# Sparse attention, then a layer-normed feed-forward block: a new order for the prologue and for each batch's attention pieces

## Chip, cores and metric

The kernel runs on one core of one Trainium2 chip. The metric is the device time of one execution in microseconds (us). Before the change it is 962.87 us, the median of three runs (959.76 to 963.36).

## The reference

Attention with 8 batches, 8 heads, 576 tokens and 64 values to a head. Heads 0 to 3 see the last 32 tokens (local), heads 4 to 7 see every 32nd token back (strided). Its result x (8 x 576 x 512) goes through a layer norm and a feed-forward block of 512 to 2048 to 512, and is added back:

```python
scores = scale * np.matmul(q, k.transpose(0, 1, 3, 2))
mask_local = (rel >= 0) & (rel < 32)
mask_strided = (rel >= 0) & (pos[None, :] % 32 == pos[:, None] % 32)
attn = softmax(np.where(masks, scores, -1e9))
x = attn @ v                                   # heads side by side: (8, 576, 512)
xn = (x - mu) / np.sqrt(var + 1e-06) * g_ln
out = x + np.maximum(xn @ w_ch1, 0.0) @ w_ch2
```

q, k and v are 32-bit floats; the two weight matrices are 64-bit floats.

## The kernel before

**Feed-forward.** The 8 x 576 tokens are cut into nine chunks of 512: chunk c below 8 is the first 512 tokens of batch c, the ninth is the 64 tokens left over from each batch. A chunk takes 16 steps f, one for each 128 columns of the hidden layer. A step has two halves on TensorE: `ffn1(c, f)` (L544) makes `ph` by 12 matmuls of 128x512 out of x and the first weights; ScalarE and VectorE turn `ph` into the two parts `hh` (L559) and `hl` (L560); `ffn2(c, f)` (L564) adds 12 more matmuls into the four outputs `po`. Everything is held as a high and a low part, hence three products for each. In the loop `ffn2` runs one step late: step f does `ffn1(c, f)`, an attention piece, `ffn2(c, f - 1)`. In chunk 0 there is one PSUM bank for `ph`; from chunk 1 on, when the bank of the weight preparation `ps_r` is given back, there are two. `finish` (L574) ends a chunk: it scales `po` with the row statistics `rs`, adds x and stores.

**Weights.** All weights stay in SBUF, and they are prepared on the way, one step's worth (`Split(f)`, L180) at a time: `scaled`, `low` (ScalarE), `magnitude`, `sign` (VectorE) turn 64-bit words into floats; `by_g`, `chunks_sum` (GpSimd) scale by g and sum over rows; `column_mean` (TensorE, L227, the tile `cm`) and `centred` (VectorE, L230) take off the column mean, which is the layer norm's mean; `two_parts` (ScalarE L241, GpSimd L242) makes high and low parts. During chunk 0 three splits are in work at a time: in step f the old one (f + 1) is ended, the next (f + 2) is in its middle, the one after (f + 3) is begun. Chunk 0 is the only chunk that carries this work.

**Attention.** A batch is four pairs of heads, in the order local, strided, local, strided; pair i of 32 belongs to batch i // 4. A pair goes through a turn (`t_piece`, L347: VectorE transposes q and k; `turned(i)`, L671, then issues the load of pair i + 1 on the SP queue) and four pieces: s (scores on TensorE into the one two-bank tile `ps_a`; mask L394, maximum L401 on VectorE; subtraction L406 on GpSimd; later the exponential L411 on ScalarE), p (transposes, copy L419), v (times v, L430 or L439; division L445 to L451 on VectorE; stores and the load of the next v on the SP queue), x (transposes L472 into `px`, split into the tiles `xh` L489 and `xl` L491 that the next chunk's `ffn1` reads). Below s5 is the s piece of pair 5. The generator `pieces` (L677) strings them as s(i+1), v(i), p(i+1), x(i), one for each step, across the batches' borders; a chunk's x must be ended when the chunk begins. Steps 0 and 1 of chunk 0 take no piece, so steps 12 to 15 take two each (L785 to L787), and chunk 0 takes 18 in all: s4 and p4, then up to s8, v7, p8, x7. The 32nd pair's x comes accordingly two steps before the end of chunk 6. Turns in chunk 0 stand at steps 0, 3, 5, 7, 8, 12, 14 (pairs 4 to 10).

**Prologue.** Batch 0's four pairs a, b, c, d (b and d strided) have no chunk to hide in. Lines 609 to 662 write out their order by hand, with the splits of weights 0 and 1 put between them. `t_rows` (L307) does the turn on TensorE, and four copies each on ScalarE and VectorE put the result in place (L325 local, L330 strided: 288 values to a row, written 36 values apart). Three two-bank tiles are handed round (`bank`, L249).

Each engine runs its instructions in the order in which they are written; a dependency at the end (L801 to L811) keeps it so.

## Time and profile before

| | |
|---|---|
| median of three runs | 962.87 us (959.76 to 963.36) |
| the profiled execution | 962.91 us |
| its span, first to last instruction | 961.1 us |
| TensorE busy | 923.6 us, 96% |
| VectorE / ScalarE / GpSimd busy | 391.5 / 225.2 / 143.1 us |
| mean granted clock of TensorE | 0.986 |

The profiled execution lies within 0.04 us of the median, and 1.8 us of it lie outside the span. Busy shares are means over the whole run; the tables of the busy tenths show VectorE, ScalarE and GpSimd at 5 to 8 tenths in the first sixth of the span, where the prologue and chunk 0 lie, and at 1 to 4 tenths after it, with TensorE at 9 or more. So the run has two parts that have to be read apart.

### The profile page before, as it was taken

The page shows a single profiled execution, that of the slowest core. Times are in us where ns is not written, and L with a number is a line of the kernel's source. Part 1 is how long each engine was busy: PE and PEld are TensorE (multiplying, and loading weights), DVE is VectorE, ACT ScalarE, POOL GpSimd, SP SyncE. Part 2 cuts the span into 40 slices and gives each one's busy share as a digit, 9 for nine tenths or more (in the row PEclk, how much of TensorE's full clock was granted, in tenths as well). Part 3 has the DMA queues.
Part 4 walks back from the last instruction along what each step waited for, and adds up shares of the span by engine and source line. Part 5 has one row for each costly group of instructions (what it writes and reads, how often), then busy time and mean ns, then how long its engine had stood idle before and what let it go on. Part 6 is the DMA issues. An engine that isn't in the chain of part 4 may idle for free.

```text
span 961.1 us, 18676 instructions
## 1 busy us (share of the span) xinstructions
PE 923.6 (96%) x7984; PEld 752.8 (78%) x7984; DVE 391.5 (41%) x685; ACT 225.2 (23%) x375; POOL 143.1 (15%) x180
## 2 busy tenths in 40 slices
PE   6679889999999999999999999999999999999996
PEld 5558677888888888888888888888888888888885
DVE  6668785433442344333442344334422321122112
ACT  5467562212121111121112111211112111101100
POOL 3368664000100010000000010001000000000000
PEclk9799998999999999999999999999999999999999
DMA  9997954524334242414432434243311121002001
GB/s 195 246 233 189 196 156 88 135 52 74 76 84 75 47 87 79 75 40 92 105 63 51 95 63 105 52 92 65 81 27 38 34 92 40 1 1 88 0 1 44
DMA packets 241666, 80.72 MB, mean 84 GB/s; under 512 B 192304, under 2 KB 234928, under 8 KB 241584
## 3 DMA queue, kind: packets, MB, share of 16 engines
q1 hardware_dynamic: 238688, 78.35, 36.1%
q10 hardware_dynamic: 2896, 1.18, 0.7%
q8 instruction: 63, 1.03, 0.5%
q14 instruction: 19, 0.16, 0.1%
HBM read 60.03 MB, written 19.46 MB: 83 GB/s over the span
## 4 chain that ended last, share of the span: by engine, by line
PE 88%; DVE 4%; issue 3%; POOL 2%; ACT 1%; DMA 1%; SPq 1%; DVEq 0%; ACTq 0%; POOLq 0%
PE po L570 40%; PE ph L551 26%; PE ph L555 13%; PE pp L416 2%; PE px L472 1%; PE av L430 1%; PE sp L375 1%; PE av L439 1%; PE sp L387 1%; DVE p L200 1%; SPq L292 1%; POOL w L242 1%; DVE r L206 1%; DVE kt_s L330 1%; DMA rows<-in_k_dram 1%
## 5 line engine op out<-in xcount | busy, mean ns | idle before, releaser
L570 PE MATMUL po<-w,hh 128*128 128x512 f32 x1152 | 367.5, 400 | 0.5 <-ACT hh L559 0.5
L560 DVE SCALAR_TENSOR_TENSOR hl<-ph,hh 128x512 fp32r<-128x512 f32 x144 | 99.6, 692 | 490.2 <-ACT hh L559 490.2
L570 PEld LDWEIGHTS po<-w,hh 128*128 128x128 f32 x1152 | 208.1, 188 | 43.3 <-ACT hh L559 0.7
L551 PE MATMUL ph<-xh,w 128*128 128x512 f32 x576 | 229.0, 398 | 0.0
L551 PE MATMUL ph<-xl,w 128*128 128x512 f32 x576 | 226.9, 394 | 0.0
L570 PE MATMUL po<-w,hl 128*128 128x512 f32 x576 | 225.6, 392 | 0.0
L559 ACT ACTIVATE hh<-ph 128x512 fp32r<-128x512 f32 x144 | 85.9, 596 | 567.8 <-PE ph L555 567.4
L555 PE MATMUL ph<-xh,w 128*128 128x512 f32 x576 | 155.6, 392 | 0.0
L570 PEld LDWEIGHTS po<-w,hl 128*128 128x128 f32 x576 | 108.1, 188 | 24.8 <-DVE hl L560 0.4
L551 PEld LDWEIGHTS ph<-xh,w 128*128 128x128 f32 x576 | 109.6, 190 | 22.6
L555 PEld LDWEIGHTS ph<-xh,w 128*128 128x128 f32 x576 | 109.3, 190 | 23.0
L551 PEld LDWEIGHTS ph<-xl,w 128*128 128x128 f32 x576 | 109.8, 191 | 22.3
L406 POOL TENSOR_TENSOR sm<-sm,mx 128x640 f32<-128x640 f32 (+1 forms) x32 | 40.7, 1271 | 406.4 <-DVE mx L401 403.0
L532 POOL TENSOR_TENSOR rs<-rs,mhalf 128x1 f32<-128x1 f32 x36 | 19.8, 550 | 360.6 <-DVE rs L531 360.6
L411 ACT ACTIVATE sm<-sm 128x640 f32<-128x640 f32 (+1 forms) x32 | 23.8, 744 | 98.2 <-POOL sm L406 98.2
L242 POOL TENSOR_TENSOR w<-r,w 128x512 fp32r<-128x512 f32 x32 | 40.9, 1293 | 28.9 <-ACT w L241 27.4
L491 DVE TENSOR_TENSOR xl<-px,xh 128x512 fp32r<-128x512 f32 (+2 forms) x48 | 30.1, 658 | 17.7 <-ACT xh L489 17.7
L576 DVE SCALAR_TENSOR_TENSOR x<-po,rs,x 128x512 f32<-128x512 f32 x36 | 24.7, 746 | 18.0 <-PE po L570 18.0
L489 ACT ACTIVATE xh<-px 128x512 fp32r<-128x512 f32 (+2 forms) x48 | 27.6, 650 | 10.7 <-PE px L472 9.9
L451 DVE TENSOR_TENSOR xo<-av,den 128x640 f32<-128x640 f32 (+1 forms) x32 | 28.5, 891 | 1.1
L472 PE MATMUL px<-ident,xo 128*128 128x128 f32 x160 | 24.4, 287 | 4.0 <-DVE xo L451 3.9
L200 DVE SCALAR_TENSOR_TENSOR p<-s,p 128x512 uint32<-128x512 uint32 x32 | 22.2, 693 | 12.8 <-ACT p L195 12.7
(73 smaller groups left out, 569.8 us busy)
## 6 DMA issues: line engine op xcount, KB each, us to landing
s<-in_moe_w_ch_dram SPq DMA_DIRECT2D x32, 512.0 KB
out_dram<-x SPq DMA_DIRECT2D x32, 256.0 KB
raw<-in_q_dram SPq DMA_DIRECT2D x112, 72.0 KB
raw<-in_k_dram SPq DMA_DIRECT2D x112, 72.0 KB
xds<-xo SPq DMA_DIRECT2D x32, 162.0 KB
v_l<-in_v_dram SPq DMA_DIRECT2D x32, 144.0 KB
v_l<-in_v_dram SPq DMA_DIRECT2D x32, 136.0 KB
xdl<-xo SPq DMA_DIRECT2D x16, 256.0 KB
```

Of the source, the lines that this page charges most:

```text
L200: nc.vector.scalar_tensor_tensor(out=self.p[i], in0=self.bits[i][:, :, 1], scalar=3, in1=self.p[i], op0=ALU.logical_shift_left, op1=ALU.bi ...
L242: nc.gpsimd.tensor_tensor(out=t[:, 1], in0=w, in1=t[:, 0].bitcast(F32), op=ALU.subtract)
L406: nc.gpsimd.tensor_tensor(out=sm, in0=sm, in1=mx[:, :, 0:nt].unsqueeze(3).broadcast_to([P, 2, nt, w]), op=ALU.subtract)
L451: nc.vector.tensor_tensor(out=xo[:, 0:nt].rearrange("p t h d -> p h t d"), in0=av[:, :, :, 0:D], in1=den.unsqueeze(3).broadcast_to([P, 2, ...
L472: nc.tensor.transpose(px[:, P * t:P * (t + 1)], self.xov[:, t], ident)
L489: nc.scalar.activation(out=dst(xh), in_=src, func=AF.Copy)
L491: nc.vector.tensor_tensor(out=dst(xl), in0=src, in1=dst(xh).bitcast(F32), op=ALU.subtract)
L551: nc.tensor.matmul(ph, w1h[:, cc], x[:, cc, :], start=(n == 0), stop=False)
L555: nc.tensor.matmul(ph, w1l[:, cc], xh[:, cc, :], start=False, stop=(cc == NCC - 1))
L559: nc.scalar.activation(out=hh, in_=ph, func=AF.Relu)
L560: nc.vector.scalar_tensor_tensor(out=hl, in0=ph, scalar=0.0, in1=hh.bitcast(F32), op0=ALU.max, op1=ALU.subtract)
L570: nc.tensor.matmul(po[i], hx[:, cs], w, start=(f == 0 and n == 0), stop=(f == NFC - 1 and n == 2))
```

## The change

What it does, part by part:

1. `t_rows`, strided: the copy walks the same 288 values in the other order, so that it writes runs of 18 neighbours and reads PSUM 16 values apart.
2. The prologue's order: split 0 is spread over the pairs' work (`d.s_act` earlier, `scaled(1)`, `low(1)`, `column_mean`, `centred` and `two_parts` between the p, v and x pieces), split 1 is begun before d's v piece, and its `column_mean` is done in the prologue.
3. Step 0's `ph` is begun in the prologue, pair by pair: 3 matmuls for pair a's rows ahead of d's x piece, 9 after it, in the order b, c, d.
4. Step 0 takes the turn of pair 4 and no `ffn2`; `ffn2(0, 0)` moves to step 1, behind `ffn1(0, 1)` and ahead of s4.
5. A batch's attention is 16 pieces within one chunk. In chunk 0: s4 at step 1, none at 2, p4, s5, v4, p5, x4, s6, v5, p6, x5, s7, v6 at steps 3 to 13, p7 and x6 at 14, v7 and x7 at 15. Turns at steps 0, 3, 6, 10, 14 and 15 (pairs 4 to 9; the last stands behind x7). Later chunks: one piece for each step, s, s, p, v, p, x, s, v, p, x, s, v, p, x, v, x.
6. Chunk 0's loads of x move from steps 9 to 12 to steps 11 to 14, and its row statistics from steps 11 to 14 (one each) to 14 and 15 (two each). Other chunks keep theirs.

```diff
-                            t = dst[rows, 0:S].rearrange("p (u c t) -> p c t u", c=2, t=NB)
-                            copy(out=t[:, c], in_=src.rearrange("p (t u) -> p t u", u=n))
+                            t = dst[rows, 0:S].rearrange("p (u c t) -> p c u t", c=2, t=NB)
+                            copy(out=t[:, c], in_=src.rearrange("p (t u) -> p u t", u=n))
...
+    def ffn1_part(c, f, ph, ccs):
+        xh, xl = xt[c]
+        w1h, w1l = w1_parts(f)
+        for cc in ccs:
+            for w, x in ((w1h, xh), (w1l, xh), (w1h, xl)):
+                nc.tensor.matmul(
+                    ph, w[:, cc], x[:, cc, :], start=(cc == 0 and x is xh and w is w1h),
+                    stop=(cc == NCC - 1 and x is xl))
...
-    new.scaled(0)
-    new.low(0)
-    new.scaled(1)
-    new.magnitude(0)
-    new.sign(0)
-    new.by_g()
-    new.chunks_sum()
+    s0.scaled(0)
+    s0.low(0)
+    s0.magnitude(0)
+    s0.sign(0)
+    d.s_act()
+    s0.scaled(1)
+    s0.by_g()
+    s0.chunks_sum()
     a.v_piece()
+    s0.low(1)
+    c.p_piece()
+    s0.magnitude(1)
+    s0.sign(1)
     b.v_piece()
+    d.p_piece()
+    s0.column_mean()
+    s0.centred()
+    c.v_piece()
     a.x_piece()
...
+    s0.two_parts(0)
     b.x_piece()
...
+    s1 = Split(1)
+    s1.scaled(0)
+    s1.low(0)
+    d.v_piece()
+    s1.magnitude(0)
+    s1.sign(0)
+    s0.two_parts(1)
+    s1.by_g()
+    s1.chunks_sum()
     c.x_piece()
...
+    s1.scaled(1)
+    ph0 = ffn1_ph(0, 0)
+    ffn1_part(0, 0, ph0, (0,))
     d.x_piece()
+    ffn1_part(0, 0, ph0, (2, 1, 3))
+    s1.low(1)
+    s1.magnitude(1)
+    s1.sign(1)
+    s1.column_mean()
     pairs[NHP].load_v()
     pairs[NHP + 1].load_v()
     w_late()
...
+    def pieces(i):
+        p = pairs[i:i + NHP]
+        s, t, u, x = ([getattr(p, n) for p in p] for n in ("s_piece", "p_piece", "v_piece", "x_piece"))
+        if i == NHP:
+            return [
+                (lambda: turned(i),), (s[0],), (), (t[0], lambda: turned(i + 1)), (s[1],),
+                (u[0], lambda: next_v(i + 2)), (t[1], lambda: turned(i + 2)), (x[0],), (s[2],),
+                (u[1], lambda: next_v(i + 3)), (t[2], lambda: turned(i + 3)), (x[1],), (s[3],),
+                (u[2], lambda: next_v(i + 4)), (t[3], lambda: turned(i + 4)),
+                (u[3], lambda: next_v(i + 5))], {
+                    NFC - 2: (x[2],), NFC - 1: (x[3], lambda: turned(i + 5))}
+        return [
+            (s[0],), (s[1],), (t[0], lambda: turned(i + 2)), (u[0], lambda: next_v(i + 2)),
+            (t[1], lambda: turned(i + 3)), (x[0],), (s[2],), (u[1], lambda: next_v(i + 3)),
+            (t[2], lambda: turned(i + 4)), (x[1],), (s[3],), (u[2], lambda: next_v(i + 4)),
+            (t[3], lambda: turned(i + 5)), (x[2],), (u[3], lambda: next_v(i + 5)), (x[3],)], {}
...
+        if c == 0:
+            loads = {f: [f - 11] for f in range(11, 15)}
+            scales = {14: [0, 1], 15: [2, 3]}
+        else:
+            loads = {f: [f - 9] for f in range(9, 13)}
+            scales = {f: [f - 11] for f in range(11, 15)}
...
             if c == 0 and f == 0:
-
-                h = ffn1(c, f)
-                old, new = new, Split(WAHEAD)
-                old.column_mean()
+                old, new, nxt = s1, Split(WAHEAD), Split(WAHEAD + 1)
+                old.centred()
+                old.two_parts(0)
                 new.scaled(0)
                 new.low(0)
-                new.scaled(1)
                 new.magnitude(0)
                 new.sign(0)
...
+                h = ffn1_h(0, 0, ph0)
+                new.scaled(1)
+                new.low(1)
                 old.two_parts(1)
-                ffn2(c, f, h, po)
...
+                if f == 1:
+                    h = ffn1(c, f)
+                    old.column_mean()
...
             if c == 0 and f == 1:
-                pass
-            elif c + 1 < B:
-
-                next(gen, None)
+                ffn2(c, 0, prev, po)
+            if work:
+                for w in work[f]:
+                    w()
...
-            if prev is not None:
+            if prev is not None and (c or f > 1):
                 ffn2(c, f - 1, prev, po)
-            if c == 0 and f >= NFC - WAHEAD - 2:
-                exps()
-                next(gen, None)
-            if new:
+            for w in more.get(f, []):
+                w()
+            if new and f:
                 new.column_mean()
```

## Rows read from the trace of the kernel before

**Rows 1.** Span and clock of the core: us, mean granted clock.
```profile
core 0: 961.1 us, clock 0.986
```

**Rows 2.** Busy time by step: edges, length, PE PEld DVE ACT POOL (instructions), clock, DMA, GB/s.
```profile
43.59:56.65 13.06, 8.34 (x31) 6.06 (x29) 7.86 (x13) 7.63 (x14) 6.02 (x8) 0.87 0.91 231
56.65:62.72 6.07, 4.81 (x16) 3.56 (x16) 3.51 (x6) 2.68 (x5) 5.62 (x6) 0.72 1.07 227
62.72:70.23 7.51, 7.18 (x109) 5.45 (x108) 5.98 (x10) 5.63 (x10) 5.06 (x6) 1.00 0.93 270
...
76.53:83.29 6.76, 6.76 (x77) 5.44 (x76) 5.98 (x9) 4.19 (x8) 4.80 (x5) 1.00 0.59 93
83.29:90.18 6.89, 6.89 (x110) 5.53 (x108) 6.02 (x12) 5.25 (x9) 6.10 (x7) 1.00 0.84 300
102.75:109.91 7.16, 7.14 (x110) 5.45 (x108) 6.32 (x11) 3.98 (x8) 4.80 (x5) 1.00 1.02 241
109.91:120.12 10.21, 7.20 (x76) 5.46 (x76) 7.25 (x12) 5.32 (x10) 6.01 (x6) 1.00 0.90 179
120.12:132.92 12.80, 12.80 (x65) 10.50 (x65) 9.45 (x15) 9.55 (x18) 9.61 (x10) 1.00 0.88 244
132.92:143.61 10.69, 8.16 (x156) 6.45 (x156) 9.77 (x17) 5.30 (x9) 6.58 (x7) 0.95 0.17 51
143.61:154.85 11.24, 9.73 (x38) 7.71 (x38) 5.33 (x11) 3.79 (x6) 5.24 (x6) 0.74 0.80 146
154.85:162.58 7.73, 7.73 (x155) 6.00 (x154) 4.87 (x10) 1.46 (x3) 4.31 (x4) 1.00 0.01 2
162.58:172.18 9.60, 9.60 (x54) 7.98 (x48) 4.38 (x10) 2.86 (x5) 0.55 (x1) 1.00 0.61 115
172.18:273.39 101.21, 101.21 (x939) 82.36 (x938) 40.40 (x70) 18.46 (x30) 7.29 (x8) 1.00 0.36 76
```

**Rows 3.** TensorE in order of time: start, length, what, [idle before, releaser].
```profile
27.70 0.98 PE L430 MATMUL av<-v_l,pt 64*32 64x65 f32 x49 [3.12 <-issue]
...
56.40 0.49 PE L227 MATMUL cm<-sum,mean 128*128 128x128 f32 x2 [4.25 <-POOL sum L222]
...
114.56 1.03 PE L439 MATMUL av<-v_s,pt 54*64 54x65 f32 x48 [1.64 <-DVE r L230]
...
119.91 0.46 PE L227 MATMUL cm<-sum,mean 128*128 128x128 f32 x2 [1.37 <-DVE xo L451]
...
143.19 0.77 PE L227 MATMUL cm<-sum,mean 128*128 128x128 f32 x2 [2.53 <-DVE xo L451]
...
157.78 1.04 PE L375 MATMUL sp<-kt_l,qt_l 64*32 64x64 f32 x80
...
165.46 0.71 PE L416 MATMUL pp<-ident,sm 128*128 128x128 f32 x5
...
178.78 1.04 PE L430 MATMUL av<-v_l,pt 64*32 64x65 f32 x80
```

**Rows 4.** VectorE in order of time, in steps 9 and 15 of chunk 0.
```profile
113.16 0.78 DVE L352 STREAM_TRANSPOSE kt_l<-raw 128x576 f32<-128x576 f32 x1 [1.66 <-DMA raw<-in_k_dram]
...
170.78 1.20 DVE L491 TENSOR_TENSOR xl<-px,xh 128x480 fp32r<-128x480 f32 x2 [3.74 <-ACT xh L489]
```

**Rows 5.** VectorE by line and shape, 0 to 200 us: count, busy us, mean ns, idle before.
```profile
L330 DVE COPY kt_s<-t 64x288 f32<-64x288 f32 x8 | 5.4, 669 | 1.9 <-PE t L315 1.8
L356 DVE STREAM_TRANSPOSE qt_s<-raw 128x576 f32<-128x576 f32 x4 | 5.0, 1248 | 0.0
L394 DVE TENSOR_TENSOR sm<-sp,mask_s 128x648 f32<-128x648 f32 x5 | 4.1, 828 | 0.2
L325 DVE COPY kt_l<-t 64x288 f32<-64x288 f32 x8 | 3.6, 454 | 4.9 <-PE t L315 4.9
L527 DVE BATCH_NORM_STATS2 st<-x 128x6 f32<-128x512 f32 x4 | 2.8, 690 | 0.0
L576 DVE SCALAR_TENSOR_TENSOR x<-po,rs,x 128x512 f32<-128x512 f32 x4 | 2.7, 740 | 0.0
```

More of the change, by code (lines that the diff above doesn't have):

```diff
@@ L541, in x_turn, with ffn1_ph, w1_parts, ffn1_h @@
         split_x(xh[:, :, cs], xl[:, :, cs], px)
+    def ffn1_ph(c, f):
+        return ps_h[f % len(ps_h)].tile([P, CH], F32, tag="h", name=f"ph{c}_{f}")
+    def w1_parts(f):
+        return [w1s[f][:, i].rearrange("p (c f) -> p c f", c=NCC) for i in range(2)]
+    def ffn1_part(c, f, ph, ccs):
[6 more added lines that the diff above has]
+                    stop=(cc == NCC - 1 and x is xl))
+    def ffn1_h(c, f, ph):
+        hh = hp_.tile([P, CH], F32R, tag="hh", name=f"hh{c}_{f}")
+        hl = hp_.tile([P, CH], F32R, tag="hl", name=f"hl{c}_{f}")
+        nc.scalar.activation(out=hh, in_=ph, func=AF.Relu)
+        nc.vector.scalar_tensor_tensor(
+            out=hl, in0=ph, scalar=0.0, in1=hh.bitcast(F32), op0=ALU.max, op1=ALU.subtract)
+        return hh, hl
     def ffn1(c, f):
         xh, xl = xt[c]
-        ph = ps_h[f % len(ps_h)].tile([P, CH], F32, tag="h", name=f"ph{c}_{f}")
-        w1h, w1l = (w1s[f][:, i].rearrange("p (c f) -> p c f", c=NCC) for i in range(2))
+        ph = ffn1_ph(c, f)
+        w1h, w1l = w1_parts(f)
         n = 0
@@ L556, in ffn1 @@
                 ph, w1l[:, cc], xh[:, cc, :], start=False, stop=(cc == NCC - 1))
-        hh = hp_.tile([P, CH], F32R, tag="hh", name=f"hh{c}_{f}")
-        hl = hp_.tile([P, CH], F32R, tag="hl", name=f"hl{c}_{f}")
-        nc.scalar.activation(out=hh, in_=ph, func=AF.Relu)
-        nc.vector.scalar_tensor_tensor(
-            out=hl, in0=ph, scalar=0.0, in1=hh.bitcast(F32), op0=ALU.max, op1=ALU.subtract)
-        return hh, hl
+        return ffn1_h(c, f, ph)
     def ffn2(c, f, h, po):
@@ L606 @@
         w_load(f)
-    new = Split(0)
+    s0 = Split(0)
     a.t_rows()
@@ L664 @@
     w_late()
-    banks[:] = [(ps_a, "a")]
     NP = len(pairs)
@@ L675, in turned, with next_v @@
                 pairs[i + 1].load_qk()
-    def pieces():
-        pairs[NHP].s_piece()
-        yield
-        pairs[NHP].p_piece()
-        turned(NHP + 1)
-        yield
-        for i in range(NHP, NP):
-            if i + 1 < NP:
-                pairs[i + 1].s_piece()
-                if i > NHP:
-                    turned(i + 3)
-                yield
-            pairs[i].v_piece()
-            if i + 2 < NP:
-                pairs[i + 2].load_v()
-            if i == NHP:
-                turned(i + 2)
-            yield
-            if i + 1 < NP:
-                pairs[i + 1].p_piece()
-                yield
-            pairs[i].x_piece()
-            if i == NHP:
-                turned(i + 3)
-            yield
-    gen = pieces()
+    def next_v(i):
+        if i < NP:
+            pairs[i].load_v()
+    def pieces(i):
[14 more added lines that the diff above has]
+            (t[3], lambda: turned(i + 5)), (x[2],), (u[3], lambda: next_v(i + 5)), (x[3],)], {}
+    new = nxt = None
     for c in range(NCHUNK):
+        banks[:] = [(ps_a, "a")]
         po2 = [ps_o.tile([P, 1024], F32, tag="o", name=f"po{c}_{i}") for i in range(NT // 2)]
@@ L708 @@
         if c == 1:
-            exps()
-            new = nxt = None
             ps_r_ctx.close()
@@ L713 @@
                 tc.tile_pool(name="ps_h1", bufs=1, space=bass.MemoryType.PSUM)))
+        work, more = pieces(NHP * (c + 1)) if c + 1 < B else ([], {})
+        if c == 0:
[4 more added lines that the diff above has]
+            scales = {f: [f - 11] for f in range(11, 15)}
         prev = None
@@ L720 @@
             if c == 0 and f == 0:
[L722 to L724 removed]
+                old, new, nxt = s1, Split(WAHEAD), Split(WAHEAD + 1)
+                old.centred()
+                old.two_parts(0)
                 new.scaled(0)
                 new.low(0)
[L727 removed]
                 new.magnitude(0)
                 new.sign(0)
[L730 to L733 removed]
+                h = ffn1_h(0, 0, ph0)
+                new.scaled(1)
+                new.low(1)
                 old.two_parts(1)
[L735 to L736 removed]
                 new.magnitude(1)
[L738 to L746 removed]
+            elif c == 0:
                 old, new, nxt = new, nxt, Split(f + WAHEAD + 1) if f + WAHEAD + 1 < NFC else None
+                if f == 1:
+                    h = ffn1(c, f)
+                    old.column_mean()
                 if old:
@@ L759 @@
                     new.magnitude(1)
-            h = ffn1(c, f)
+                if f > 1:
+                    h = ffn1(c, f)
+            else:
+                new = nxt = None
+                h = ffn1(c, f)
             if new:
```

45 lines of the change are left out of this document (3 added, 42 removed).

## The prediction, made before the changed kernel ran

> **What bounds the kernel now.** I read the span first: 961.1 us with the clock at 0.986 [rows 1], so TensorE is nearly always at its upper level of 2.4 GHz and there is little to win from the clock as a whole. Then the busy times of the page: TensorE works 923.6 us, so it is idle for 37.5. The next question is where, and for that I cut the span at the start of each step's first `ffn1` matmul [rows 2]. The reader is to see two kinds of rows. Chunk 1, a stretch of 101.21 us with 16 pieces, has TensorE busy for all of it, and VectorE at 40.40: there nothing but TensorE counts, and a piece costs its own length wherever it stands. Chunk 0 is different. Its undisturbed steps take 6.76 (with a strided s) and 6.89 us (with a local v) and are TensorE's too; but steps 0 to 2 last 13.06, 6.07 and 7.51 us, step 9 lasts 10.21, and steps 12, 13, 14 last 10.69, 11.24 and 7.73. What they have beyond 6.8 or so is lost, and the change is made in just these places.
>
> The waits say why [rows 3]. In step 1 TensorE stands 4.25 us for the sum of split 2 on GpSimd. In step 9 it stands 1.64 and 1.37 us for VectorE, and VectorE's own row shows that it had stood 1.66 us for the k that pair 8's turn transposes [rows 4]: all that is queued behind the turn (`centred`, the bit work of the next split, v5's division) came late. In step 13 (143.19) it is 2.53 us behind a VectorE that is busy for 9.77 of step 12's 10.69 us: two pieces, a strided turn and the statistics in one step. After this gap the clock of step 13 reads 0.74, so a part of it ran at 1.2 GHz.
>
> **The change, part by part.** The sum is made against the profiled execution, 962.91 us, which is the median of the three runs to 0.04.
>
> *The copies of `t_rows`.* They take 0.669 us where written 36 values apart and 0.454 where written 2 apart [rows 5], 288 values both times. The new order makes the write dense and the PSUM read sparse; no row shows such a read. Ends: 0.454 (the whole difference is the write's; 8 copies on VectorE, 1.7 us less) and 0.88 (the read costs as much again; 1.7 more). I take 0.669, the row of the line itself. What is won here is largely swallowed: all these copies are done by 23 us, and TensorE then stands inside a's v piece for 3.12 us with no releaser, to 27.70 [rows 3]. So the term is 0.
>
> The Trainium skill (Advanced Engine Details and Errata, PSUM Cachelines) says that PSUM is accessed in lines of two 32-bit values and that every two consecutive elements should be neighbours. By that rule the read would take back what the write gives and the sum would have the same 0; the rows show the cost of a sparse write only.
>
> *Prologue, step 0's `ph`, steps 0 to 2.* The three windows last 26.64 us, TensorE is busy for 20.33 of them. Step 0's `ph` no longer runs as 12 matmuls after the last x: 3 stand ahead of it, 6 wait for earlier pairs. Split 1 gets its mean in the prologue. That brings `ph` and split 1 some 3 to 4 us forward, by laying the new order out along each queue. But the lead melts: `hl` of step 0 now stands behind split 2's `magnitude` and `sign` on VectorE, `ph` has one bank, so `ffn1(0, 1)` waits for `hl`, and split 2's column mean now stands behind `ffn1(0, 1)`, which after this idle stretch runs again at 1.2 GHz, as in step 1 of before (clock 0.72). From split 2's mean to the start of step 3 GpSimd has to do two splits (4.80 us each, the step with the strided s) and s4's subtraction (1.3, from 6.10 in the step beside it), 10.9 us at the least; before it was 56.40 to 70.23. s4 comes one step earlier, so its subtraction lies inside this stretch again. I take 1.2 us gained at the start of step 3. Ends: 4.2 gained (the whole wait of step 1 goes), 1.5 lost (no lead, and s4's subtraction delays split 4).
>
> *Steps 3 to 8.* Pieces as before; the turns are spread wider. Step 8 loses pair 8's turn and should last 6.89 rather than 7.16: 0.3 gained.
>
> *Step 9.* The turn that waited for its k is gone; the next one (pair 7) stands at step 10, four steps after its load was released, where pair 8's was released one step before. So 10.21 becomes 6.89: 3.3 gained. Its loads of x move to step 11, behind which they free the SP queue for the weights.
>
> *Steps 10 and 11.* Same pieces, 12.80 us for both. VectorE has 9.45 us here and gets pair 7's turn, 2 x 1.25 [rows 5]: 11.95. The cover is thus 0.85 us; gone, it costs up to 1. Term 0.
>
> *Steps 12 to 14.* They were 10.69 + 11.24 + 7.73 = 29.66. They now carry s7; v6; p7 and x6, with one turn, no s8, no v7, and statistics only in step 14. I price them by the clean steps: 6.76, 6.89, and 6.9 for step 14, which has two short pieces but no column mean. Sum 20.55: 9.1 gained, with no idle gap for the clock to fall in. Ends: 4.5 (half of it) and 9.5.
>
> *Step 15.* v7 (about 0.95) for p8 (0.71) [rows 3]: 9.9 for 9.60, 0.3 lost.
>
> *s8 and p8* are not saved; they run in later chunks, where TensorE is full. At 1.04 and 0.71 of overlapping busy time [rows 3] that is at most 1.75; I take 1.5 lost.
>
> *The border to chunk 1: a new wait.* Behind x7's `xl`, which ends 0.2 us before chunk 1 begins [rows 4], VectorE now has pair 9's turn (2.5), two bn_stats (1.4), `finish` (4 x 0.74, overlapping to 2.7), `hl` of chunk 1's step 0 (0.7) and s8's mask (0.83) [rows 5]. s8's scores leave the only `ps_a` tile then, 7.9 us after the border. TensorE wants that tile for s9 in step 1, 6.6 us after the border (178.78 against 172.18). It waits 1.3, with the small followers of bn_stats 1.5. Ends: 0 and 4 (if pair 9's k, loaded only one step earlier, is late as in step 9). In chunks 2 to 6 neither turn nor statistics stand there, and 2.6 us are to spare.
>
> **Sum:** -1.2 - 0.3 - 3.3 + 0 - 9.1 + 0.3 + 1.5 + 1.5 = -10.6. 962.91 - 10.6 = 952.3 us.
>
> **Rivals.**
> *VectorE stays the bound of chunk 0.* It keeps six of seven turns and all of the splits, with 0.85 us to spare in steps 10 and 11. Then half of steps 12 to 14 comes back (4.5 rather than 9.1) and half of step 9's wait returns at step 10 (1.7): 952.3 + 6.3 = 958.6. For it: step 12's 9.77 of 10.69. Against it: step 12 loses v6 and a turn, and steps 4 and 5, with the same mix as the new 12 and 13, have VectorE at 5.98 and 6.02 of 6.8.
> *The head gives more:* the copies are fast and the lead survives to step 3 (3.0 us more), and the border costs nothing (1.5): 947.8. For it: step 1 alone holds 4.25 us of pure waiting. Against it: the one bank of `ph`.
> *Slower: the wait at the border in every chunk.* The new order puts two s pieces into steps 0 and 1 of each chunk 1 to 6, both through `ps_a`; the old order had a v piece there. If VectorE lets go of `ps_a` late in chunks 2 to 6 as well, each microsecond is paid five times. The change is slower by over 0.5% from 3.1 us in each of the five, 967.7; at 3.4 it is 969. For it: my own sum has it in chunk 1. Against it: VectorE would have to be 2.6 + 3.1 us later than reckoned, while it is busy for 40% of such a chunk.
> *A part that does nothing:* the copies may stay at 0.67; that is already the sum.
>
> **How the numbers follow.** Chances: the forecast 0.60, VectorE still the bound 0.18, the head gives more 0.16, slower 0.06. The forecast's own range is 948 to 957, from the ends of the head, of steps 10 and 11 and of the border. To leave out no more than 2 in 10 I go from 946.5 to 959: below lie 0.05 of the better case, above 0.08 of the VectorE case and the 0.06. A measurement of this kernel can tell about 0.5% from no change, 4.8 us: faster means below 958.1. That holds the forecast nearly whole, the better case and a third of the VectorE case: 0.81. Slower, above 967.7, is 0.05 of the last case; the rest, 0.14, is the same.
>
> **What would show it.** Step starts 6.3 to 7 us apart from step 3 to step 14, TensorE without idle there, clock 1.00; step 9 without a wait for raw k; chunk 0 from the start of step 3 to chunk 1 in about 90 us rather than 102; a wait of TensorE for VectorE's mask in step 1 of chunk 1 and nowhere else; the strided copies at 0.67. I am wrong if VectorE is busy over 95% in steps 10 to 14 with TensorE waiting for it, if step 3 begins after 70.2, or if chunks 2 to 6 last longer than 101.2.

## The result, and the profile after

The changed kernel takes 950.4 us, the median of four runs (949.45 to 950.83); the kernel before, run beside it, takes 962.88 (959.76 to 963.36). The ratio is 0.9876, with an interval of 0.9854 to 0.9898: 12.5 us less, against 10.6 forecast. The profiled execution took 949.45 us.

The page of the changed kernel gives the span and the busy time of each engine; the row of the cores gives the clock.

```profile
span 947.4 us, 18698 instructions
...
PE 916.7 (97%) x7984; PEld 747.8 (79%) x7984; DVE 388.9 (41%) x685; ACT 223.2 (24%) x375; POOL 143.4 (15%) x180
```
```profile
core 0: 947.4 us, clock 0.993
```

The span is 13.6 us shorter than in [rows 1] (961.05 and 947.45 to the hundredth). TensorE is busy for 916.7 us of it and idle for 30.7; it was idle for 37.5. So 6.7 of the 13.6 are idle time, and the other 6.9 are busy time; the plainest piece of it is step 13, which kept TensorE busy for 9.73 us at a clock of 0.74 [rows 2].

Busy time by step of the changed kernel, cut at each step's first `ffn1` matmul, with the columns of [rows 2]. The first line is the end of the prologue from the first `ph` matmul on, with step 0; then follow steps 1, 2, 9, 10 and 11 together, 12, 13, 14, 15, and the whole of chunks 1 and 2.

```profile
36.75:47.62 10.87, 4.67 (x21) 2.90 (x22) 8.55 (x16) 6.80 (x14) 4.81 (x5) 0.83 0.97 317
47.62:58.72 11.10, 8.81 (x108) 6.74 (x109) 7.78 (x13) 6.56 (x13) 8.26 (x9) 0.86 0.89 195
58.72:65.81 7.09, 5.98 (x29) 4.66 (x28) 4.35 (x7) 5.29 (x10) 6.10 (x7) 1.00 1.00 205
...
105.20:112.00 6.80, 6.80 (x78) 5.45 (x76) 5.20 (x9) 4.79 (x8) 5.90 (x7) 1.00 0.38 135
112.00:125.15 13.15, 12.90 (x66) 10.49 (x65) 11.03 (x16) 9.55 (x17) 9.60 (x10) 1.00 0.84 179
125.15:131.91 6.76, 6.76 (x77) 5.45 (x76) 5.49 (x8) 4.50 (x8) 4.94 (x6) 1.00 0.22 66
131.91:138.81 6.90, 6.90 (x110) 5.53 (x108) 5.06 (x9) 3.13 (x5) 6.74 (x7) 1.00 0.01 4
138.81:145.42 6.61, 6.61 (x37) 5.50 (x36) 2.72 (x4) 2.03 (x3) 1.66 (x2) 1.00 0.89 173
145.42:155.50 10.08, 10.08 (x93) 8.18 (x92) 5.92 (x14) 2.31 (x4) 1.11 (x2) 1.00 0.63 130
155.50:257.97 102.47, 101.25 (x939) 82.38 (x938) 44.16 (x78) 18.33 (x30) 8.38 (x10) 1.00 0.40 82
257.97:359.18 101.21, 101.21 (x940) 82.39 (x938) 39.43 (x69) 18.45 (x30) 7.28 (x8) 1.00 0.36 75
```

Step 9 was 10.21 and is 6.80; steps 12 to 14 were 29.66 and are 20.27. In all four TensorE's busy time equals the length, and the clock is 1.00 where step 13 had 0.74. In steps 10 and 11, 0.25 us are idle; in chunk 1, 1.22, and by this it lasts 102.47 us rather than 101.21. Chunks 2 to 6 last 101.21 each, as chunk 1 did before; only chunk 6, which carried two pieces fewer before, took 99.39 then.

Those gaps have a name in TensorE's timeline, which also shows the ones left in the head (columns as in [rows 3]):

```profile
26.70 0.86 PE L430 MATMUL av<-v_l,pt 64*32 64x65 f32 x49 [2.78 <-issue]
...
47.62 0.79 PE L575 MATMUL ph<-xh,w 128*128 128x512 f32 x1 [4.84 <-DVE hl L564]
...
58.48 0.49 PE L227 MATMUL cm<-sum,mean 128*128 128x128 f32 x2 [2.29 <-DVE sm L399]
...
65.56 0.49 PE L227 MATMUL cm<-sum,mean 128*128 128x128 f32 x2 [1.11 <-POOL sum L222]
...
124.94 0.46 PE L227 MATMUL cm<-sum,mean 128*128 128x128 f32 x2 [0.25 <-DVE xl L491]
...
163.52 0.92 PE L387 MATMUL sp<-kt_s,qt_s 64*64 64x54 f32 x48 [1.22 <-DVE sm L394]
```

The row at 47.62 is `ffn1(0, 1)` waiting for `hl` of step 0 and so for the one bank of `ph`. The row at 58.48 names VectorE (a MEMSET of s4's piece), but GpSimd's sum of split 3 ends within 0.02 us of it (58.42 and 58.44): the two came last together. The row at 163.52 is s9 in step 1 of chunk 1, waiting for s8's mask.

Put beside each other, span by span, the terms of the sum are these:

| stretch | before | after | difference | forecast |
|---|---|---|---|---|
| start of the span to step 3 | 70.23 | 65.81 | -4.42 | -1.2 (copies 0) |
| steps 3 to 8 | 39.68 | 39.39 | -0.29 | -0.3 |
| step 9 | 10.21 | 6.80 | -3.41 | -3.3 |
| steps 10 and 11 | 12.80 | 13.15 | +0.35 | 0 |
| steps 12 to 14 | 29.66 | 20.27 | -9.39 | -9.1 |
| step 15 | 9.60 | 10.08 | +0.48 | +0.3 |
| chunk 1 to the end | 788.87 | 791.94 | +3.07 | +3.0 |
| sum | 961.05 | 947.45 | -13.6 | -10.6 |

Seven terms, and six of them hold to 0.4 us or better. All that was missed lies ahead of step 3.

The table compares one execution of each kernel, and two of its rows change from execution to execution, so that hits to the tenth are in part luck. Four more kernels below have the same head up to step 3 (border_all, border_early, stats_back, turns_back) and begin step 3 at 65.82, 66.61, 66.65 and 67.77 us: against 70.23 the head gains 2.5 to 4.4 us, and the 4.42 of the table is the best of five. And the 29.66 us of steps 12 to 14 hold the step 13 whose clock read 0.74. In copies_only, where the clock stayed at 1.00, the same steps of the old order take 26.93 us, and the gain would be 6.7.

### The profile page after: what moved, and what is told of

Read it like the earlier page. It is cut to its first block, busy times and chain, and to the rows that moved or that the text cites. A ratio compares the mean times of both kernels' runs of the same rounds, so it can differ in the third digit from the quotient of the medians.

```text
span 947.4 us, 18698 instructions
## 1 busy us (share of the span) xinstructions
PE 916.7 (97%) x7984; PEld 747.8 (79%) x7984; DVE 388.9 (41%) x685; ACT 223.2 (24%) x375; POOL 143.4 (15%) x180
## 4 chain that ended last, share of the span: by engine, by line
PE 92%; DVE 3%; DMA 2%; issue 1%; ACT 1%; SPq 1%; DVEq 0%; POOL 0%; POOLq 0%; ACTq 0%
PE po L589 41%; PE ph L575 27%; PE ph L579 13%; PE pp L416 2%; PE av L430 2%; PE px L472 2%; PE sp L387 2%; PE sp L375 1%; PE av L439 1%; DMA rows<-in_k_dram 1%; DMA raw<-in_q_dram 1%; DVE p L200 1%; PE t L315 1%; DVE r L206 1%; DVE x L595 0%
## 5 line engine op out<-in xcount | busy, mean ns | idle before, releaser
L575 PE MATMUL ph<-xh,w 128*128 128x512 f32 x572 | 225.7, 395 | 4.8 <-DVE hl L564 4.8
L575 PE MATMUL ph<-xl,w 128*128 128x512 f32 x572 | 223.6, 391 | 0.0
L579 PE MATMUL ph<-xh,w 128*128 128x512 f32 x572 | 153.3, 390 | 0.0
L575 PEld LDWEIGHTS ph<-xh,w 128*128 128x128 f32 x572 | 108.0, 189 | 27.4 <-DVE hl L564 5.0
L579 PEld LDWEIGHTS ph<-xh,w 128*128 128x128 f32 x572 | 107.4, 188 | 22.4
L200 DVE SCALAR_TENSOR_TENSOR p<-s,p 128x512 uint32<-128x512 uint32 x32 | 22.2, 693 | 12.3 <-ACT p L195 12.2
L401 DVE TENSOR_REDUCE mx<-sm 128x10 f32<-128x640 f32 (+1 forms) x32 | 26.4, 824 | 2.1
```

The costliest lines, as they stand in the source:

```text
L200: nc.vector.scalar_tensor_tensor(out=self.p[i], in0=self.bits[i][:, :, 1], scalar=3, in1=self.p[i], op0=ALU.logical_shift_left, op1=ALU.bi ...
L401: nc.vector.reduce_max(mx[:, :, 0:nt], sm, axis=AX.X)
L575: nc.tensor.matmul(ph, w1h[:, cc], x[:, cc, :], start=(n == 0), stop=False)
L579: nc.tensor.matmul(ph, w1l[:, cc], xh[:, cc, :], start=False, stop=(cc == NCC - 1))
```

## The experiments

Twelve kernels ran in four groups; the kernels of a group share a chip and the runs of the kernel before. Differences of a few tenths of a per cent lie near the width of these intervals, and the text says where only a trace shows a thing.

| kernel | median us (range, runs) | before | ratio (95%) |
|---|---|---|---|
| copies_only | 959.93 (957.82 to 962.56, 12) | 962.17 | 0.9976 (0.9963 to 0.9989) |
| all_but_copies | 952.73 (952.17 to 953.53, 6) | 962.17 | 0.9903 (0.9887 to 0.9919) |
| pieces_only | 954.46 (953.75 to 955.49, 6) | 962.17 | 0.9921 (0.9904 to 0.9938) |
| head_only | 959.26 (957.13 to 962.33, 12) | 962.17 | 0.9967 (0.9953 to 0.9982) |
| border_early | 948.63 (948.05 to 949.08, 4) | 961.32 | 0.9866 (0.9851 to 0.9881) |
| border_all | 950.0 (949.47 to 951.23, 4) | 961.32 | 0.9885 (0.9868 to 0.9901) |
| head_order | 949.84 (949.24 to 951.1, 4) | 961.32 | 0.988 (0.9866 to 0.9895) |
| both | 948.18 (947.12 to 949.59, 4) | 961.32 | 0.9862 (0.9847 to 0.9878) |
| turns_back | 953.44 (951.29 to 954.89, 6) | 962.46 | 0.9903 (0.9882 to 0.9923) |
| stats_back | 948.98 (948.55 to 950.39, 5) | 962.46 | 0.9862 (0.984 to 0.9883) |
| chain | 947.78 (947.4 to 949.21, 4) | 961.87 | 0.9853 (0.9834 to 0.9872) |
| chain_head | 947.86 (947.35 to 948.06, 5) | 961.87 | 0.985 (0.9832 to 0.9869) |

### The change in its parts

**The copies alone**, in the kernel before:

```diff
-                            t = dst[rows, 0:S].rearrange("p (u c t) -> p c t u", c=2, t=NB)
-                            copy(out=t[:, c], in_=src.rearrange("p (t u) -> p t u", u=n))
+                            t = dst[rows, 0:S].rearrange("p (u c t) -> p c u t", c=2, t=NB)
+                            copy(out=t[:, c], in_=src.rearrange("p (t u) -> p u t", u=n))
```

> The kernel before with the new walk of the strided copies and nothing else. Theory (the copies are 0.454 us by the profile of the changed kernel, and the front up to a's v piece is a chain through them): the resumption of a's v piece comes about 1 us earlier and the whole run is 0.5 to 1.5 us shorter, about 961.9 us against 962.9. Rival (the wait of TensorE inside a's v piece and the chain of split 2 swallow it, as the forecast had it): 962.9 within 0.4, with steps 1 and 2 beginning where they did.

It wins 2.24 us (0.11 to 0.37%), more than the 0.5 to 1.5 expected. The rows of the changed kernel by line and shape, 0 to 200 us (count, busy us, mean ns, idle before; VectorE first, then ScalarE), give the price of the copies:

```profile
L330 DVE COPY kt_s<-t 64x288 f32<-64x288 f32 x8 | 3.6, 454 | 2.2 <-PE t L315 2.2
L325 DVE COPY kt_l<-t 64x288 f32<-64x288 f32 x8 | 3.6, 455 | 5.4 <-PE t L315 5.3
...
L330 ACT COPY qt_s<-t 64x288 f32<-64x288 f32 x8 | 3.2, 395 | 0.4 <-PE t L315 0.2
L325 ACT COPY qt_l<-t 64x288 f32<-64x288 f32 x8 | 3.3, 411 | 4.1 <-PE t L315 3.9
```

L330 reads PSUM 16 values apart and L325 does not, and they cost the same. So what the 0.669 in [rows 5] had above 0.454 was the cost of the sparse write. Over 8 copies VectorE saves 8 x 0.215 = 1.7 us, ScalarE, whose strided copies took 0.663 before, 8 x 0.268 = 2.1, and the median of the whole kernel gains about that.

Where it gains them, the trace of copies_only alone does not show. TensorE stops in a's v piece 1.2 us earlier than before (23.39 against 24.58), but stands there for 4.41 us instead of 3.12, to 27.80 instead of 27.70; in this execution the stall did swallow the lead, against the expectation. Step 3 begins 0.72 us earlier (69.51 against 70.23), and 3.3 of this execution's 4.0 us lie in steps 9 to 14, 2.7 of them in steps 12 to 14, where the clock did not fall here. Over all profiled kernels the lead does pass: with the old copies the stall ends at 27.70, 28.33 (pieces_only) and 28.89 (all_but_copies), with the new ones between 25.89 and 28.31, at 26.9 in the mean of eleven.

**All but the copies**: the changed kernel with the two lines above put back.

> The changed kernel with the old walk of the strided copies. Theory: copies back at 0.67 us, front about 1 us later, and nothing after it gives the microsecond back, since TensorE is full from step 3 on: 951.0 to 951.9 us against 950.4. Rival (swallowed): 950.4 within 0.4.

Its ratio is 0.0027 above that of the changed kernel, 2.6 us of 962; up to 1.5 was expected. The two estimates of the copies, in the old order 2.2 and in the new 2.6, agree; the first lies outside no change by its own interval, the second is the difference of two that overlap.

**The pieces alone**: the copies, the prologue and step 0 of before, and the new string of pieces, turns, loads and statistics. s4 stands at step 2, the first that takes a piece there.

```diff
-    gen = pieces()
...
+        work, more = pieces(NHP * (c + 1)) if c + 1 < B else ([], {})
...
-                next(gen, None)
+                for w in work[f]:
+                    w()
...
+                (), (), (s[0],), (t[0], lambda: turned(i + 1)), (s[1],),
```

> The kernel before, its prologue, copies and step 0 untouched, with the new 16 pieces of a batch, the new turns and the new places of chunk 0's statistics; s4 stays at step 2. Theory (the terms of steps 3 to 15 and of the later chunks are independent of the head): 0.3 + 3.4 - 0.35 + 9.4 - 0.5 - 3.0 = 9.3 us less than before, 953.6 us, with step 9 at 6.8 and steps 12 to 14 together at 20.3. Rival (the new steps hold only because the head runs ahead of the weights' preparation): steps 9 to 14 keep waits for VectorE or GpSimd, and less than 5 us are won.

It wins 7.7 us by the median and 8.7 in the span, where the terms from step 3 on sum to 9.3. Its windows for step 9, and for steps 12 to 14 together:

```profile
110.17:116.96 6.79, 6.79 (x78) 5.44 (x76) 5.20 (x9) 4.80 (x8) 5.88 (x6) 1.00 0.43 156
...
130.11:150.38 20.27, 20.27 (x216) 16.48 (x216) 13.29 (x21) 9.65 (x16) 13.35 (x13) 1.00 0.36 82
```

These are the lengths of the changed kernel to 0.01 us (6.80 and 20.27). From step 3 to chunk 1 it takes 89.69 us, the changed kernel 89.69, the kernel before 101.95. What it wins in chunk 0 does not hang on the head; in the profiled execution its step 3 began 0.5 us later than before. What else its median lacks of 9.3 is not resolved; the 9.3 counts a step 13 with the clock at 0.74, and not every execution of the old order has that (see copies_only). VectorE, busy for 13.29 of 20.27 us, does not bound these steps: that rival falls.

**The head alone**: the new copies, prologue and steps 0 and 1, and the old string of pieces, so that two stand in each of steps 12 to 15.

```diff
-                for w in work[f]:
-                    w()
+            if c == 0 and f < 2:
+                if f == 0:
+                    turned(NHP)
+            elif c + 1 < B:
+                next(gen, None)
...
+            if c == 0 and f >= NFC - WAHEAD - 2:
+                exps()
+                next(gen, None)
```

> The changed kernel's prologue, copies and steps 0 and 1 with the old string of pieces (18 in chunk 0), old turns from pair 5 on and old statistics. Theory: step 3 begins 4 to 4.5 us earlier than before (near 66), and the waits of steps 9 and 12 to 14 come back unchanged, since they hang on the distance of turns and pieces in steps: 958 to 959 us. Rival (the waits are for transfers whose time does not move with the head): the lead is eaten at step 9, 961.5 us or more.

Its median is 959.26, a little above the 958 to 959 expected. The stalls of [rows 2] are back at steps 9, 12 and 13:

```profile
108.46:118.48 10.02, 7.17 (x77) 5.47 (x76) 7.21 (x12) 5.33 (x10) 6.01 (x6) 1.00 0.92 181
131.26:141.75 10.49, 7.99 (x156) 6.24 (x156) 9.57 (x17) 5.33 (x9) 6.57 (x7) 1.00 0.21 68
141.75:151.93 10.18, 8.68 (x38) 6.91 (x38) 5.50 (x11) 3.80 (x6) 5.27 (x6) 0.83 0.90 161
```

From step 3 to chunk 1 it takes 100.50 us, where the kernel before takes 101.95. Step 3 begins at 68.74, not near 66 as expected; s4 stands in step 2 here, and that step takes 8.30 us at a clock of 0.82, against 7.09 at 1.00 in the changed kernel.

Against copies_only it has the new prologue with steps 0 and 1 more, and its median is 0.7 us lower, which ranges as wide as these do not tell from nothing. All_but_copies against pieces_only has the same more, with s4 a step earlier, and is 1.7 lower, with ranges that do not overlap. So the new order of the head is worth something, and the forecast's 1.2 lies between the two.

### Step 9 and the turns

The turns of pairs 7 and 8 go back to steps 7 and 8:

```diff
-                (u[0], lambda: next_v(i + 2)), (t[1], lambda: turned(i + 2)), (x[0],), (s[2],),
-                (u[1], lambda: next_v(i + 3)), (t[2], lambda: turned(i + 3)), (x[1],), (s[3],),
-                (u[2], lambda: next_v(i + 4)), (t[3], lambda: turned(i + 4)),
+                (u[0], lambda: next_v(i + 2)), (t[1], lambda: turned(i + 2)), (x[0], lambda: turned(i + 3)), (s[2], lambda: turned(i + 4)),
+                (u[1], lambda: next_v(i + 3)), (t[2],), (x[1],), (s[3],),
+                (u[2], lambda: next_v(i + 4)), (t[3],),
```

> The changed kernel with two turns back where they were: pair 7's at step 7, pair 8's at step 8, one step after its load is released. Theory (step 9's 3.4 us were the turn that waited for its own raw k, with all of VectorE's work queued behind it): step 9 lasts 9 to 10.5 us again, 2.5 to 3.7 us more than the changed kernel, about 953.5 us. Rival (step 9 was long because the transfers of steps 8 to 10 as a whole were too many, turns, x loads and weights together; with the x loads gone to step 11 the k is in time): under 1 us more.

Steps 8 and 9 of this kernel, and VectorE's turn in step 9:

```profile
100.30:108.25 7.95, 7.19 (x109) 5.45 (x108) 6.79 (x11) 3.95 (x8) 4.79 (x5) 1.00 0.91 190
108.25:117.76 9.51, 7.20 (x77) 5.47 (x76) 7.16 (x12) 5.32 (x10) 6.00 (x6) 1.00 0.99 187
```
```profile
110.80 0.78 DVE L352 STREAM_TRANSPOSE kt_l<-raw 128x576 f32<-128x576 f32 x1 [1.19 <-DMA raw<-in_k_dram]
```

The wait for the raw k of [rows 4] is there again, 1.19 us, and with it a step of 9.51. From step 3 to chunk 1 it takes 93.14 us, 3.45 more than the changed kernel; the ratio is 0.0027 higher, 2.6 us. Steps 8 and 9 together take 17.46 us here, 17.37 before and 13.68 in the changed kernel. The gain is thus the turns' spacing; moving the loads of x to step 11, which this kernel keeps, does not bring it.

### The border to chunk 1

**The two statistics of step 15 ahead of x7**, in chunk 0 alone:

```diff
+            if c == 0 and f == NFC - 1:
+                for i in scales.pop(f):
+                    xres[i].append(x_scale(xres[i][0], f"{c}_{i}"))
             for w in more.get(f, []):
                 w()
```

> The changed kernel with chunk 0's last two row statistics ahead of x7 in step 15 instead of behind it; there VectorE stands idle for 2.9 us. Theory (the wait of 1.22 us at s9 is the length of VectorE's queue behind x7): the queue is 2.0 us shorter, the wait is gone, 1.2 us less than the changed kernel, about 949.2 us. Rival (the wait hangs on pair 9's transfer or on finish alone): the wait stays near 1.2, 950.4.

VectorE's queue at the border in the changed kernel, where chunk 1 begins at 155.50, and then in this one, where it begins at 156.36:

```profile
154.11 1.22 DVE L491 TENSOR_TENSOR xl<-px,xh 128x480 fp32r<-128x480 f32 x2 [2.92 <-ACT xh L489]
...
157.40 0.64 DVE L527 BATCH_NORM_STATS2 st<-x 128x6 f32<-128x512 f32 x1
...
159.41 2.73 DVE L595 SCALAR_TENSOR_TENSOR x<-po,rs,x 128x512 f32<-128x512 f32 x4
162.06 0.68 DVE L564 SCALAR_TENSOR_TENSOR hl<-ph,hh 128x512 fp32r<-128x512 f32 x1
162.65 0.81 DVE L394 TENSOR_TENSOR sm<-sp,mask_l 128x640 f32<-128x640 f32 x1
```
```profile
155.01 1.20 DVE L491 TENSOR_TENSOR xl<-px,xh 128x480 fp32r<-128x480 f32 x2
...
158.28 2.64 DVE L595 SCALAR_TENSOR_TENSOR x<-po,rs,x 128x512 f32<-128x512 f32 x4
160.84 0.68 DVE L564 SCALAR_TENSOR_TENSOR hl<-ph,hh 128x512 fp32r<-128x512 f32 x1
161.43 0.81 DVE L394 TENSOR_TENSOR sm<-sp,mask_l 128x640 f32<-128x640 f32 x1
```

The mask begins 7.15 us after the border in the one and 5.07 in the other, by just the two statistics. TensorE's row of s9 in this kernel has no wait:

```profile
163.11 0.92 PE L387 MATMUL sp<-kt_s,qt_s 64*64 64x54 f32 x48
```

Chunk 1 lasts 101.21 us again, and from chunk 1 to the end it takes 790.69 us, 1.26 less than the changed kernel. That is the border's term. The other 1.8 of the 3.07 us that the later chunks lost are in chunk 6, which has to carry two pieces more than before, the price of s8 and p8: 101.21 against 99.39, just above the forecast's bound of 1.75. Its median is 1.4 below that of border_all, which keeps chunk 1's wait.

**The statistics as early as in the other chunks**, with their loads:

```diff
-            loads = {f: [f - 11] for f in range(11, 15)}
-            scales = {14: [0, 1], 15: [2, 3]}
+            loads = {f: [f - 9] for f in range(9, 13)}
+            scales = {f: [f - 11] for f in range(11, 15)}
```

> The changed kernel with chunk 0's x loads back at steps 9 to 12 and its row statistics back at steps 11 to 14. Theory: the border to chunk 1 loses its wait (1.2 us less), while steps 11 to 13 get 1.05 us of VectorE each where the cover is under 1 us, and lose about 1: 950.4 within 0.7, the wait moved from the border to steps 11 to 13. Rival (the x loads hold up the weights on the SP queue): split 14 or 15 comes late, 2 us or more lost in steps 11 to 13.

The wait at the border is gone here too: 790.67 us from chunk 1 to the end. What this puts back into steps 12 and 13 costs little:

```profile
126.02:132.78 6.76, 6.76 (x77) 5.44 (x76) 5.92 (x12) 4.25 (x8) 5.28 (x6) 1.00 0.62 134
132.78:139.84 7.06, 7.06 (x110) 5.45 (x108) 6.16 (x13) 3.25 (x6) 6.51 (x7) 1.00 0.08 27
```

Step 13 is 0.16 longer, where about 1 us was expected to be lost in steps 11 to 13, and from step 3 to chunk 1 it takes 89.88 us, 0.2 more. So moving the x loads and statistics of chunk 0, taken alone, costs about 1 us: once the turns and pieces were spread, VectorE had room for them where they were. The medians say the same (0.9862 against 0.9876), but within their intervals.

**The same queue at the border of every chunk**: turn and the last two statistics behind the last x in chunks 1 to 6 too, to try the rival that ended slower.

```diff
-            (t[3], lambda: turned(i + 5)), (x[2],), (u[3], lambda: next_v(i + 5)), (x[3],)], {}
+            (t[3],), (x[2],), (u[3], lambda: next_v(i + 5)), (x[3],)], {NFC - 1: (lambda: turned(i + 5),)}
...
-            scales = {f: [f - 11] for f in range(11, 15)}
+            scales = {f: [f - 11] for f in range(11, 15)} if c + 1 >= B else {11: [0], 12: [1], 15: [2, 3]}
```

> The changed kernel with the same load at the borders of chunks 2 to 6 as at chunk 1's: the second strided turn of a batch and the last two statistics stand behind the batch's last x. Theory (in-order VectorE in front of the one ps_a tile): each of five borders shows a wait of 1.0 to 1.6 us of TensorE in step 1, 5 to 8 us more than the changed kernel, 956 to 958 us; VectorE's busy share does not change. Rival (those borders have 2.6 us to spare and swallow it): 951.5 or less.

It takes 950.0 us, 6 to 8 less than expected, and 791.90 from chunk 1 to the end, where the changed kernel takes 791.94. VectorE at the border to chunk 2, which begins at 258.01, and TensorE at the strided s behind it:

```profile
253.93 1.19 DVE L491 TENSOR_TENSOR xl<-px,xh 128x480 fp32r<-128x480 f32 x2 [0.51 <-ACT xh L489]
...
261.84 0.68 DVE L564 SCALAR_TENSOR_TENSOR hl<-ph,hh 128x512 fp32r<-128x512 f32 x1
262.44 0.81 DVE L394 TENSOR_TENSOR sm<-sp,mask_l 128x640 f32<-128x640 f32 x1
```
```profile
264.75 0.92 PE L387 MATMUL sp<-kt_s,qt_s 64*64 64x54 f32 x48
```

The same border in the changed kernel, without turn and statistics:

```profile
256.89 2.76 DVE L595 SCALAR_TENSOR_TENSOR x<-po,rs,x 128x512 f32<-128x512 f32 x4 [1.81 <-PE po L589]
261.52 0.69 DVE L564 SCALAR_TENSOR_TENSOR hl<-ph,hh 128x512 fp32r<-128x512 f32 x1 [1.87 <-ACT hh L563]
```

The longer queue, and no wait. The reason is the first row of border_all: in later chunks the last x stands ahead of `ffn2` of the step before, and in chunk 0 x7 stands behind it. So `xl` begins 1.4 us before the border in chunk 0 (154.11 against 155.50), and in the changed kernel's next border 4.1 us before (253.89 against 257.97). That gives VectorE 2.7 us more. Turn and statistics still push `finish` from 256.89 to 259.20, but in the changed kernel VectorE has 1.87 us idle behind `finish`, and this takes most of it up: the mask begins only 0.31 us later (262.44 against 262.13). The slower rival would have needed both a longer queue and a late x.

### What is left in the head

**Step 0's order**: `hh` and `hl` of step 0 and split 1's second half ahead of split 2's work.

```diff
+                h = ffn1_h(0, 0, ph0)
+                old.two_parts(1)
                 new.scaled(0)
...
-                h = ffn1_h(0, 0, ph0)
...
-                old.two_parts(1)
```

> The changed kernel with another order inside step 0: hh and hl of step 0 and the second half of split 1 ahead of split 2's first half. Theory (TensorE's 4.84 us before ffn1(0,1) hang on hl behind split 2's bit work, and ph has one bank): the wait falls to about 3 us, the sum of split 2 comes no later than now, step 3 begins 0.7 to 2 us earlier, about 949 us. Rival (GpSimd's chain of splits sets step 3): ffn1(0,1) begins earlier and the column mean of split 2 or 3 waits for the same time longer, 950.4 within 0.4.

Its median is 949.84, no gain that these runs show. The wait for `hl` shrinks from 4.84 to 2.94 us and `ffn1(0, 1)` begins at 46.59 rather than 47.62. Yet step 2 begins at 58.70 and step 3 at 65.78, where the changed kernel has 58.72 and 65.81. The lead goes into split 3's column mean:

```profile
46.59 0.74 PE L575 MATMUL ph<-xh,w 128*128 128x512 f32 x1 [2.94 <-DVE hl L564]
...
58.46 0.49 PE L227 MATMUL cm<-sum,mean 128*128 128x128 f32 x2 [2.87 <-DVE sm L399]
```

Together with border_early it is the kernel **both**:

> The last-mentioned order of step 0 together with the two statistics ahead of x7. Theory: the two gains add, 1.2 + 1.4, about 947.8 us. Rival: only the border's 1.2 is there, 949.2.

It takes 948.18 us against 948.63 for border_early alone, which is no difference. The head's end is set elsewhere.

**The chain through split 2**: border_early, and in step 1 split 2's low part ahead of `ffn1(0, 1)`'s `hh`, and `centred` ahead of `hl`.

```diff
                 if f == 1:
-                    h = ffn1(c, f)
+                    old.two_parts(1)
+                    ph1 = ffn1_mm(c, f)
                     old.column_mean()
-                if old:
+                    old.centred()
+                    h = ffn1_h(c, f, ph1)
+                    old.two_parts(0)
+                elif old:
                     old.two_parts(1)
                     old.centred()
                     old.two_parts(0)
```

> The changed kernel with the two statistics ahead of x7 (as in border_early) and, in step 1, the second half of split 2 ahead of ffn1(0,1)'s hh, and split 2's centring ahead of hl. Theory (the chain of splits on GpSimd sets the start of step 3; GpSimd stood idle for 1.42 us before split 2's low part, which waited for ScalarE behind hh): the column mean of split 3 comes about 1 us earlier after ffn1(0,1)'s start, and so does step 3; 947.6 us where border_early had 948.6. Rival (TensorE's own start of ffn1(0,1) and the slow clock there set it): step 3 does not move, 948.6.

GpSimd's low part, which in the changed kernel stood idle for 1.42 us before 53.33, follows the sum at once:

```profile
50.40 0.46 POOL L222 TENSOR_TENSOR sum<-sum 128x128 f32<-128x128 f32 x1
50.81 1.29 POOL L242 TENSOR_TENSOR w<-r,w 128x512 fp32r<-128x512 f32 x1
53.27 1.30 POOL L242 TENSOR_TENSOR w<-r,w 128x512 fp32r<-128x512 f32 x1 [1.17 <-ACT w L241]
```

But the next one now waits 1.17 us for ScalarE. Split 3's sum on GpSimd ends at 56.91, and its column mean begins only at 57.47:

```profile
57.47 0.52 PE L227 MATMUL cm<-sum,mean 128*128 128x128 f32 x2 [1.93 <-DVE sm L394]
```

In the changed kernel GpSimd's sum and s4's piece on VectorE came last together; here GpSimd is 0.55 us early, and the mask of s4, which ends at 57.32, comes last by the profile. So speeding up GpSimd alone wins little. Step 3 begins 18.47 us after step 1; in the changed kernel it is 18.19, in border_early 19.41. At 947.78 us it is 0.9 below border_early, within the intervals. Whether this order wins anything is left open. With head_order's step 0 as well it is **chain_head**:

> The same with step 0's order of head_order besides. Theory: now that split 2 no longer waits behind hh, the earlier ffn1(0,1) counts: another 0.5 to 1 us, 947.0 us. Rival: ffn1(0,1) still ends at the same time because it runs at 1.2 GHz for longer, nothing more than chain.

It takes 947.86 us, the same as chain. These two, at ratios of 0.9853 and 0.985, are the fastest kernels measured here; against the changed kernel they are 2.2 and 2.5 us ahead by the ratios, of which 1.26 is the border and shown, and the rest is not resolved.

## Why the prediction was right, and where a term was off

**Direction and mechanism held, and the size lies within the range**: the measured 950.4 is 1.9 below the forecast. Steps 9 and 12 to 14 gave 12.8 us (12.4 forecast), by the ways named: turns_back brings step 9 back with its wait for raw k, head_only brings the waits of steps 9, 12 and 13 back, pieces_only takes them all away without the head. Two of the waits are named a step late: the 4.25 us at 56.40 end step 0's window, and the 2.53 us at 143.19 step 12's; no term rests on that.

**Step 9** (3.3 forecast, 3.41 measured). Right, cause and size.

**Steps 12 to 14** (9.1, measured 9.39). Pricing them by the clean steps worked: 6.76 and 6.90 came out to the hundredth, and step 14 is 6.61 where 6.9 was taken. The other side of the difference is luck in part: it holds the 2.7 us that step 13 took in this execution and did not in that of copies_only, so that 6.7 to 9.4 is what the traces show.

**Steps 10 and 11** (0, measured +0.35). TensorE waits 0.25 us at 124.94 for VectorE, as the bound of 1 allowed, but not because VectorE is full: it is busy for 11.03 of 13.15 us, not 11.95. What counted is when `xl` came in its queue, not its idle time over two steps.

**Later chunks** (1.5 for s8 and p8, 1.5 for the border; measured 1.82 and 1.26). The wait stands on the instruction that was named, in the chunk that was named, and in no other. That the sum comes out is luck: the two errors cancel. The overlapping busy times of s8 and p8 turned out to be paid in full.

**The order of the prologue** (1.2). The medians with and without it differ by 0.7 us, which is not resolved, and by 1.7, which is. Right within what these runs resolve, and two of its grounds are in the trace: `ffn1(0, 1)` does wait for `hl` (4.84 us), and split 3's mean waits for GpSimd, though s4's piece on VectorE ends with it. That the lead melts behind split 2's mean is not: this mean begins 4.44 us earlier than before (51.96 against 56.40), and from there to step 3 it takes 13.85 us, as before (13.83). The 10.9 us was a floor, and not reached.

**The step that failed is the copies' term.** It was 0, on two grounds. The first was the price, and it fell: 0.669 was taken, "the row of the line itself", and the copies took 0.454, the lower end. That row's cost belonged to the sparse write, which the change removes; the row nearest to a dense write was L325's. The second was that the gain is "largely swallowed" by TensorE's stall in a's v piece, which was read as ending at 27.70 whatever came before. It is no fixed point in time. With the same new prologue and copies the stall ends at 26.70 in the changed kernel, 25.89 in border_early, 26.18 in border_all, 27.35 in stats_back and 28.31 in turns_back, and is between 2.50 and 4.70 us long. In a single execution it can swallow the lead, as in copies_only; over the executions the medians won 2.24 and 2.6 us. A stall that the profile gives no releaser is no cover to cost anything at nothing by; what this one follows stands in the last section.

Counted from the first of `t_rows`' matmuls, step 3 begins after 66.3 us before and 65.0 in copies_only, single executions both. The 1.7 us of the rows lies between this 1.3 and the 2.24 of the medians, and inside their interval (1.1 to 3.6). With -1.7 for it the sum would have been -12.3, 950.6 us.

The Trainium skill (Advanced Engine Details and Errata, PSUM Cachelines) says that every two consecutive elements in PSUM should be neighbours for the best throughput, and the prediction took a slower read from that. For copies the runs disagree: on VectorE one that reads PSUM 16 values apart took 0.454 us beside 0.455 for L325's, and on ScalarE 0.395 beside 0.411. The measurement decides; matmuls with such a read were not tried.

**The rivals.** VectorE as the bound of chunk 0 fell with pieces_only. Of the better head, the first half came true, fast copies and a lead that is kept to step 3; the second, a border that costs nothing, did not. The slower one fell with the changed kernel's chunks 2 to 6, 101.21 us each, and border_all shows why. The part that was to do nothing, the copies, does something. Another part does harm: moving chunk 0's loads of x and statistics costs 1.26 us at the border and saves 0.16 in step 13.

## What to carry to other kernels

Price a step of an order written by hand by a step of the same mix that has no wait, and the new step comes out to tenths; the old step, where its length hangs on the clock, wants more than one execution. Then look for the place where what was moved meets the next shared buffer, because the bill comes there. When an instruction is queued ahead of another, compare the whole queue at each border, its start time as well as its length: the same queue cost 1.22 us at one border and nothing at five others, where the last x stood ahead of `ffn2` instead of behind it. A changed access pattern has two sides, so look for a row that shares the side that remains, and never let an unexplained stall hide a saving.
